# Loading the last two experts' w2 in column halves, and storing half of four output blocks before the second half arrives

## The chip, the cores and the metric

The kernel runs on one core of a Trainium2 chip. The metric is device time in microseconds (us), as the median of many executions. The profile shows one execution; its span is about 1.8 us shorter than the time of the same run (190.8 us of 192.61 us for the kernel before).

The engines have the names of the profile: PE multiplies matrices and leaves the results in PSUM, its accumulator memory; ACT and DVE do elementwise work and copy results out of PSUM (here called evicting); POOL issues the loads and SP the stores, and 16 DMA engines carry both out. In the code, `hp` and `th` are PSUM tiles of the hidden layer, `h_sb` and `hT` its result before and after a transpose, `sop` the slot outputs in PSUM, `slot_oa` the same after the eviction, `cp` and `ob` the combined output before and after its eviction.

## The reference, cut to what matters

Sliding-window attention gives x (4608 tokens by 512 columns). A soft mixture of experts follows: 32 slots, 8 experts with 4 slots each.

```python
logits = x @ phi                        # 4608 x 32
slot_input = softmax(logits, axis=0).T @ x   # needs every token
for e in range(8):                      # w1[e]: 512 x 1024, w2[e]: 1024 x 512
    slot_out[e] = np.maximum(slot_input[e] @ w1[e], 0) @ w2[e]
out = softmax(logits, axis=1) @ slot_out     # 4608 x 512 float32, 9.44 MB
```

So there is one narrow place: the slot inputs need all tokens, the outputs need all experts. Before it the kernel loads q, k, v and 33.6 MB of weights (float32 in HBM, cast to fp16 by the load); after it, it stores 9.44 MB. Everything in this document happens in that narrow place.

## The kernel before

PE builds all 32 slot outputs in one PSUM tile `sop`, evicts it to `slot_oa` in two copies, and then combines: 36 matmuls of 512 columns, each evicted into `ob` by ACT or DVE in turn, with a store for each two of them. Loads are issued by POOL, stores by SP.

```python
def load_w(e, n):                       # n = 0, 1: w1; n = 2, 3: w2, by rows
    ...
    c = slice(4 * n - 8, 4 * n - 4)
    nc.gpsimd.dma_start(out=w2_t[e][:, c], in_=moe_w2[e].rearrange("(c p) d -> p c d", p=128)[:, c])
...
def expert_h(e):                        # hidden layer
    ...                                 # 16 matmuls hp <- slot_inT, w1 (256 columns)
    nc.scalar.activation(h_sb[:, :], hp[:, :], AF.Relu)
    ...                                 # 2 matmuls th: transpose of h
    nc.vector.tensor_copy(out=hT[...], in_=th[:, :])

def expert_o(e):                        # second layer, 8 matmuls of 512 columns
    for i in range(NFC // 4):
        for g in range(4):
            nc.tensor.matmul(sop[32 * g:32 * g + 32, :], hT[:, 4 * i + g, :], w2_t[e][:, 4 * i + g, :],
                             start=(e == 0 and i == 0), stop=(e == E - 1 and i == NFC // 4 - 1))

expert_h(0)
for e in range(E):
    if e + 1 < E:
        expert_h(e + 1)
    expert_o(e)
nc.scalar.copy(out=slot_oa[:, 0:256], in_=sop[:, 0:256])
nc.vector.tensor_copy(out=slot_oa[:, 256:512], in_=sop[:, 256:512])

for blk in range(B + 1):
    ob = pw1.tile([128, 4, D], FP32, name="ob", tag="w1s")
    for g in range(4):
        ...                             # cp <- ET, slot_oa; scaled into ob[:, g, :]
    ...                                 # 2 stores of 512 KB, in rows of 2048 B
```

The softmax here doesn't subtract the row's maximum and nothing guards it: scores larger than these inputs give would overflow.

Of the kernel before, what the change touches and what calls it, by code (L numbers as in the profile page):

```python
# [8 lines left out]
FP32 = mybir.dt.float32  # L9
# [7 lines left out]
def kernel(  # L17
# [10 lines left out]
    nc = tc.nc  # L28

    B, H, S, Dh = q.shape  # L30
    D, NSLOT = moe_phi.shape
    E, _, F = moe_w1.shape
    SPE = NSLOT // E
# [14 lines left out]
    pw1 = ctx.enter_context(tc.tile_pool(name="pw1", bufs=8))  # L48
# [16 lines left out]
        loaded[u] = tiles  # L65

    w1_t, w2_t = {}, {}

    def load_w(e, n):
        if n == 0:  # L70
            w1_t[e] = pw1.tile([128, NHD, F], FP16, name="w1s", tag="w1s")
        if n == 2:
            if e < E - 1:
                w2_t[e] = pw2.tile([128, NFC, D], FP16, name="w2s", tag="w2s")
            else:
                w2_t[e] = pxb.tile([128, NFC, D], FP16, name="w2l", tag="x_bp")
        if n < 2:
            c = slice(2 * n, 2 * n + 2)
            nc.gpsimd.dma_start(out=w1_t[e][:, c], in_=moe_w1[e].rearrange("(c p) f -> p c f", p=128)[:, c])  # L79
        else:  # L80
            c = slice(4 * n - 8, 4 * n - 4)
            nc.gpsimd.dma_start(out=w2_t[e][:, c], in_=moe_w2[e].rearrange("(c p) d -> p c d", p=128)[:, c])  # L82
# [15 lines left out]
    for h in range(2):  # L98
        nc.vector.tensor_copy(
            out=rep[64 * h:64 * h + 64, :, :],  # L100
            in_=ident[64 * h:64 * h + 64, 64 * h:64 * h + 64].unsqueeze(1).broadcast_to([64, 8, 64]))
# [21 lines left out]
    ET = const.tile([128, 4 * B + B // 2, 128], FP16, name="ET")  # L123
# [4 lines left out]
    slot_oa = const.tile([128, D], FP16, name="slot_oa")  # L128
# [178 lines left out]
            nc.vector.tensor_tensor(out=acc[:, :], in0=pa[:, :], in1=acc[:, :], op=ALU.add)  # L307

    nu = len(units)
    w_order = [(e, n) for e in range(E) for n in range(4)]  # L310

    def issue_loads(u):
        if u + 3 < nu:
            load_unit(u + 3)
            for _ in range(2 if u % 3 == 2 else 1):
                load_w(*w_order.pop(0))

    load_w(*w_order.pop(0))
    load_unit(2)
    todo = []  # L320
# [3 lines left out]
    for u in range(nu):  # L324
        issue_loads(u)
        if u == nu - 3:
            while w_order:
                load_w(*w_order.pop(0))
        for j in range(3):
            stage_t2(u, j)  # L330
            stage_s(u, j)
            if u + 1 < nu:
                stage_t1(u + 1, j)
            if pend is not None:
                stage_av(*pend)
                pu, pj = pend
                if pj == 2 and units[pu][1] == 1:
                    b = units[pu][0]
                    todo += [lambda b=b: stage_xt(b, 0), lambda b=b: stage_xt(b, 1), lambda b=b: stage_xt(b, 2),
                             lambda b=b: stage_logit(b), lambda b=b: stage_ex(b), lambda b=b: stage_slot(b)]  # L340
            pend = (u, j)
            if todo:
                todo.pop(0)()
# [18 lines left out]
    ps2 = ctx.enter_context(tc.tile_pool(name="ps2", bufs=2, space=bass.MemoryType.PSUM, reuse_waits="tile"))  # L362
# [3 lines left out]
    nc.vector.tensor_copy(out=slot_inT, in_=si)  # L366

    sel = ident[:, :].rearrange("p (g s) -> p g s", s=NSLOT)
    sop = ps2.tile([128, D], FP32, name="sop", tag="sop", bufs=1)

    def expert_h(e):
        hp = ps2.tile([128, 256], FP32, name="hp", tag="hp")
        for dc in range(NHD):
            for g in range(4):
                nc.tensor.matmul(hp[32 * g:32 * g + 32, :], slot_inT[:, dc, :],
                                 w1_t[e][:, dc, 256 * g:256 * g + 256],
                                 start=(dc == 0), stop=(dc == NHD - 1))
        h_sb = pet.tile([128, 256], FP16, name="h_sb", tag="h_sb")
        nc.scalar.activation(h_sb[:, :], hp[:, :], AF.Relu)
        th = ps2.tile([128, 2, 4, SPE], FP32, name="th", tag="th", bufs=1)  # L380
        for f in range(2):
            nc.tensor.matmul(th[:, f], h_sb[:, 128 * f:128 * f + 128],
                             sel[:, :, SPE * e:SPE * e + SPE], start=True, stop=True)
        hT = hTs[e % 2]
        if e >= 2:
            nc.vector.memset(hT[:, :, SPE * (e - 2):SPE * (e - 2) + SPE], 0.0)
        nc.vector.tensor_copy(
            out=hT[:, :, SPE * e:SPE * e + SPE].rearrange("p (g f) s -> p f g s", f=2), in_=th[:, :])

    def expert_o(e):  # L390
        hT = hTs[e % 2]
        for i in range(NFC // 4):
            for g in range(4):
                nc.tensor.matmul(sop[32 * g:32 * g + 32, :], hT[:, 4 * i + g, :], w2_t[e][:, 4 * i + g, :],
                                 start=(e == 0 and i == 0), stop=(e == E - 1 and i == NFC // 4 - 1))

    expert_h(0)
    for e in range(E):
        if e + 1 < E:
            expert_h(e + 1)  # L400
        expert_o(e)
    nc.scalar.copy(out=slot_oa[:, 0:256], in_=sop[:, 0:256])
    nc.vector.tensor_copy(out=slot_oa[:, 256:512], in_=sop[:, 256:512])

    for blk in range(B + 1):
        ob = pw1.tile([128, 4, D], FP32, name="ob", tag="w1s")
        for g in range(4):
            cp = ps2.tile([128, D], FP32, name="cp", tag="cp", bufs=4)
            nc.tensor.matmul(cp[:, :], ET[:, 4 * blk + g, :], slot_oa[:, :],  # L409
                             start=True, stop=True)  # L410
            cr = crcp[:, blk, g:g + 1] if blk < B else crcp[:, 2 * g + 1, 4:5]
            if g % 2 == 0:
                nc.scalar.activation(ob[:, g, :], cp[:, :], AF.Copy, scale=cr)  # L413
            else:
                nc.vector.tensor_scalar(out=ob[:, g, :], in0=cp[:, :], scalar1=cr, scalar2=None, op0=ALU.mult)  # L415
        if blk < B:
            for g in range(0, 4, 2):
                nc.sync.dma_start(
                    out=out[S * blk + 128 * g:S * blk + 128 * g + 256, :].rearrange("(c p) d -> p c d", p=128),
                    in_=ob[:, g:g + 2, :])  # L420
        else:
            for o in range(2):
                nc.sync.dma_start(
                    out=out.rearrange("(c o t) d -> o t c d", o=2, t=S)[o, 512:576],
                    in_=ob[64 * o:64 * o + 64, :, :])


# [28 lines left out]
```

## Time and profile before

| | before |
|---|---|
| median time, 20 runs | 191.99 us |
| load queue, times of its packets summed | 94.9% of 16 engines' span |
| slot inputs ready (copy starts) | 143.69 us |
| last ReLU starts | 156.50 us |
| last w2 load lands | 158.2 us (issue 138.0, 20.2 us to landing) |
| first store issued | 161.47 us |
| first to last store packet (packet records of the trace) | 26.77 us |

The page's row of 40 slices (each 4.8 us) shows the shape: loads at about 206 GB/s until slice 32, a hole, then stores at about 380 GB/s.

```profile
DMA  4999999999999999999999999999999970999995
GB/s 69 160 201 206 208 207 206 207 210 209 208 206 207 211 206 206 207 207 212 207 205 207 208 208 207 207 211 208 210 207 211 207 118 1 361 375 380 381 339 147
```

The windows view of the kernel before shows the hole closely. Its columns are the window, its length, busy time and instruction count of each engine, then PE's granted clock as a share of the full one, the mean share of the 16 DMA engines and GB/s.

```profile
152.00:154.00 2.00, 1.35 (x32) 0.86 (x28) 0.26 (x2) 0.72 (x2) 0.00 (x0) 1.00 1.16 195
154.00:156.00 2.00, 1.67 (x41) 1.21 (x45) 0.46 (x3) 0.38 (x1) 0.00 (x0) 1.00 0.68 113
156.00:158.00 2.00, 1.51 (x28) 0.55 (x20) 0.26 (x2) 0.38 (x1) 0.00 (x0) 1.00 0.29 47
158.00:160.00 2.00, 0.82 (x6) 0.34 (x6) 0.42 (x1) 0.37 (x1) 0.00 (x0) 0.87 0.00 0
160.00:162.00 2.00, 2.00 (x6) 0.72 (x5) 1.26 (x2) 1.46 (x3) 0.00 (x0) 0.50 0.00 0
162.00:164.00 2.00, 1.80 (x6) 0.59 (x5) 1.82 (x4) 1.83 (x3) 0.00 (x0) 0.78 0.80 297
164.00:166.00 2.00, 1.80 (x7) 0.57 (x6) 2.00 (x4) 1.80 (x4) 0.00 (x0) 1.00 1.02 375
```

From 158 to 162 us nothing moves. The timeline shows what runs in that time (start, length, engine, line, operation, and in brackets how long the engine had been idle and who ended it):

```profile
143.69 0.29 DVE L366 CAST slot_inT<-si 128x128 f16<-128x128 f32 x1 [0.53 <-PE si L365]
...
156.50 0.38 ACT L379 ACTIVATE h_sb<-hp 128x256 f16<-128x256 f32 x1 [1.13 <-PE hp L375]
...
157.19 0.19 DVE L387 CAST hT_143<-th 128x32 f16<-128x32 f32 x1 [1.07 <-PE th L382]
157.44 0.40 PE L394 MATMUL sop<-w2l,hT_143 128*32 128x512 f16 x4
158.25 0.40 PE L394 MATMUL sop<-w2l,hT_143 128*32 128x512 f16 x4 [0.42 <-DMA w2l<-in_moe_w_dram]
158.70 0.37 ACT L402 CAST slot_oa<-sop 128x256 f16<-128x256 f32 x1 [1.81 <-PE sop L394]
159.10 0.42 DVE L403 CAST slot_oa<-sop 128x256 f16<-128x256 f32 x1 [1.72 <-ACT slot_oa L402]
159.58 3.72 PE L409 MATMUL cp<-slot_oa,ET 128*128 128x512 f16 x9 [0.93 <-DVE slot_oa L403]
160.21 0.69 ACT L413 ACTIVATE ob<-cp,crcp 128x512 f32<-128x512 f32 x1 [1.13 <-PE cp L409]
160.63 12.90 DVE L415 TENSOR_SCALAR ob<-cp,crcp 128x512 f32<-128x512 f32 x18 [1.10 <-PE cp L409]
161.47 19.53 SPq L418 DMA_DIRECT2D out_dram<-ob  x16
```

Two things are to be seen. The hole is a chain of short steps: second layer, two evictions one after the other, a combine, two evictions, a store. And PE waited only 0.42 us for the last load.

### The profile page before, as it was taken

To read this page: it belongs to the slowest core of one execution; us is meant where nothing else is said; L and a number is where in the kernel's file an instruction comes from. 1 tells how busy PE (TensorE), PEld (TensorE's weight loads), DVE (VectorE), ACT (ScalarE), POOL (GpSimd) and SP (SyncE) were. 2 spreads that over 40 slices of the span, in tenths; PEclk is the share of its full clock that TensorE was granted. 3 is DMA by queue.
4 is the path that set the end of the run, shared out by engine and by line. 5 is a ranking of instruction groups with operands and counts; after the bars stand their busy time and mean duration, and the time that the engine had idled before them with its cause. 6 is when DMAs were issued, how large, how long until landed. Compare 5 with 4: busy or idle time off the path is not lost.

```text
span 190.8 us, 6583 instructions
## 1 busy us (share of the span) xinstructions
PE 145.2 (76%) x2912; PEld 102.5 (54%) x2912; DVE 109.1 (57%) x259; ACT 112.3 (59%) x189; POOL 59.7 (31%) x89
## 2 busy tenths in 40 slices
PE   0499989999988799899979989988568877881000
PEld 0376767768667676676856876666324442220000
DVE  2116668687667757767766884886841123993000
ACT  2358669769587596766969669666032224992000
POOL 7944534434353434424344433332200000000000
PEclk9999999999999999999999999999955897999555
DMA  4999999999999999999999999999999970999995
GB/s 69 160 201 206 208 207 206 207 210 209 208 206 207 211 206 206 207 207 212 207 205 207 208 208 207 207 211 208 210 207 211 207 118 1 361 375 380 381 339 147
DMA packets 31308, 40.83 MB, mean 214 GB/s; under 512 B 2096, under 2 KB 22576, under 8 KB 31280
## 3 DMA queue, kind: packets, MB, share of 16 engines
q0 software_dynamic: 26384, 30.97, 94.9%
q1 hardware_dynamic: 4896, 9.44, 14.1%
q8 instruction: 23, 0.38, 0.7%
q14 instruction: 5, 0.04, 0.1%
HBM read 61.93 MB, written 9.44 MB: 374 GB/s over the span
## 4 chain that ended last, share of the span: by engine, by line
DMA 31%; PE 26%; ACT 20%; DVE 7%; issue 5%; POOL 1%; DVEq 0%; ACTq 0%; POOLq 0%
DMA w2l<-in_moe_w_dram 11%; DMA w2s<-in_moe_w_dram 9%; ACT pm L197 9%; DMA qn<-in_q_dram 8%; PE tr L143 6%; PE tr L174 5%; DVE ob L415 5%; ACT qT L150 4%; PE sc L185 3%; PE sc L192 3%; DMA kn<-in_k_dram 3%; ACT kT_125 L150 3%; PE av L220 2%; ACT kT_116 L150 2%; PE cp L409 2%
## 5 line engine op out<-in xcount | busy, mean ns | idle before, releaser
L197 ACT ACTIVATE pm<-sc 128x1024 f16<-128x1024 f32 (+1 forms) x48 | 39.5, 822 | 31.0 <-PE sc L192 30.7
L174 PE MATMUL tr<-ident,vT 128*128 128x128 f16 x288 | 24.8, 224 | 1.9 <-DVE rc L226 1.9
L150 ACT COPY qT<-tr 128x640 f16<-128x640 f16 (+1 forms) x32 | 21.8, 743 | 4.2 <-PE tr L143 4.2
L228 DVE TENSOR_TENSOR x_bp<-av,rc 128x512 f16<-128x512 f32 x32 | 21.9, 686 | 0.6
L185 PE MATMUL sc<-rep,hide 64*128 64x512 f16 (+1 forms) x96 | 20.4, 341 | 2.3 <-ACT pm L197 1.8
L174 PEld LDWEIGHTS <-vT 128*128 128x128 f16 x288 | 18.1, 100 | 6.3 <-issue 4.3
L220 PEld LDWEIGHTS <-pm 128*64 128x64 f16 x576 | 15.1, 111 | 7.5 <-issue 6.8
L175 DVE COPY vw_126<-tr 128x1024 f16<-128x1024 f16 (+1 forms) x24 | 13.4, 557 | 7.5 <-PE tr L174 6.7
L143 PE MATMUL tr<-ident,qn 128*64 128x128 f16 x288 | 12.5, 233 | 6.6 <-DMA qn<-in_q_dram 5.2
L60 POOL DMA_DIRECT2D vn<-in_v_dram x16 | 11.5, 716 | 18.5 <-PE av L220 6.4
L82 POOL DMA_DIRECT2D w2s<-in_moe_w_dram x14 | 10.6, 756 | 19.0 <-DMA w1s<-in_moe_w_dram 11.5
L79 POOL DMA_DIRECT2D w1s<-in_moe_w_dram x16 | 11.3, 708 | 16.1 <-DMA w1s<-in_moe_w_dram 7.1
L148 DVE COPY vT<-tr 128x512 f16<-128x512 f16 x16 | 11.6, 724 | 8.2 <-PE tr L143 8.1
L60 POOL DMA_DIRECT2D qn<-in_q_dram x16 | 11.5, 718 | 12.0 <-PE tr L174 3.9
L143 PE MATMUL tr<-ident,vn 128*64 128x128 f16 x288 | 13.0, 227 | 2.8 <-ACT kT_116 L150 1.4
L143 PE MATMUL tr<-ident,kn 128*64 128x128 f16 x288 | 12.0, 228 | 3.5 <-DMA kn<-in_k_dram 2.1
L60 POOL DMA_DIRECT2D kn<-in_k_dram x16 | 11.5, 716 | 9.6 <-PE tr L143 4.3
L226 DVE RECIPROCAL rc<-av 128x8 f32<-128x8 f32 x32 | 6.3, 197 | 14.1 <-PE av L220 14.1
L409 PE MATMUL cp<-slot_oa,ET 128*128 128x512 f16 x36 | 11.7, 431 | 2.3 <-ACT ob L413 1.4
L415 DVE TENSOR_SCALAR ob<-cp,crcp 128x512 f32<-128x512 f32 x18 | 12.6, 748 | 1.4 <-PE cp L409 1.1
L143 PEld LDWEIGHTS <-qn 128*64 128x64 f16 x288 | 9.5, 117 | 7.2 <-DMA qn<-in_q_dram 5.2
L175 DVE COPY vw_118<-tr 128x1024 f16<-128x1024 f16 (+1 forms) x24 | 13.2, 549 | 0.1
(97 smaller groups left out, 261.2 us busy)
## 6 DMA issues: line engine op xcount, KB each, us to landing
out_dram<-ob SPq DMA_DIRECT2D x18, 512.0 KB, 6.0
w1s<-in_moe_w_dram POOLq DMA_DIRECT2D x16, 512.0 KB, 15.1
w2s<-in_moe_w_dram POOLq DMA_DIRECT2D x14, 512.0 KB, 14.0
qn<-in_q_dram POOLq DMA_DIRECT2D x16, 288.0 KB, 13.4
kn<-in_k_dram POOLq DMA_DIRECT2D x16, 288.0 KB, 13.2
vn<-in_v_dram POOLq DMA_DIRECT2D x16, 288.0 KB, 13.2
w2l<-in_moe_w_dram POOLq DMA_DIRECT2D x2, 512.0 KB, 20.1
phi_sb<-in_moe_phi_dram POOLq DMA_DIRECT2D x1, 32.0 KB, 7.8
```

What stands on the lines that cost most here:

```text
L60: nc.gpsimd.dma_start(out=t, in_=src[b, 4 * half:4 * half + 4].rearrange("(x h) (g t) d -> (h g) x (t d)", x=2, h=2, t=T))
L143: nc.tensor.transpose(tr[64 * x:64 * x + 64, j, :], src[:, x, 64 * (t0 + j):64 * (t0 + j) + 64], ident[:, :])
L148: nc.vector.tensor_copy(out=o, in_=i)
L150: nc.scalar.copy(out=o, in_=i)
L174: nc.tensor.transpose(tr[:, 2 * w + h, :], st["vT"][:, h, 64 * i:64 * i + 128], ident[:, :])
L175: nc.vector.tensor_copy(out=st["vw"][:, wins[0]:wins[0] + n, :, 0:64], in_=tr[:, 0:2 * n, :].rearrange("p (w h) (x d) -> p w (h x) d", h=2 ...
L185: nc.tensor.matmul(sc[:, x, 0:128 * n], hide[64 * x:64 * x + 64, :], rep[64 * x:64 * x + 64, 0:2 * n, :], start=True, stop=False, skip_gro ...
L197: nc.scalar.activation(pm[:, :, 0:2 * n, :], sc[:, :, 0:128 * n].rearrange("p x (w q) -> p x w q", q=64), AF.Exp, scale=scale)
L220: nc.tensor.matmul(av[r0:r0 + 64, kk, 65 * (w // 2):65 * (w // 2) + 65], pm[:, x, h * n + w, :], st["vw"][:, i, 2 * h + x, 0:65], start=Tr ...
L228: nc.vector.tensor_tensor(out=xb[:, c0:c0 + 2, 256 * half:256 * half + 256].rearrange("p c (k d) -> p k c d", d=64), in0=avv[:, :, :, 0:64 ...
L409: nc.tensor.matmul(cp[:, :], ET[:, 4 * blk + g, :], slot_oa[:, :], start=True, stop=True)
L415: nc.vector.tensor_scalar(out=ob[:, g, :], in0=cp[:, :], scalar1=cr, scalar2=None, op0=ALU.mult)
```

## The change

The intent is to give the store queue work while the last weights still load. w2 of experts 6 and 7 is loaded by column halves, first halves first. When the first halves are in, half of each slot output is complete, and half of each row of four blocks can be combined and stored.

```diff
+    NLAST = 2
 ...
+        elif e >= E - NLAST:
+            c = slice(D // 2 * (n - 2), D // 2 * (n - 1))
+            nc.gpsimd.dma_start(out=w2_t[e][:, :, c], in_=moe_w2[e].rearrange("(c p) d -> p c d", p=128)[:, :, c])
 ...
-    w_order = [(e, n) for e in range(E) for n in range(4)]
+    w_order = [(e, n) for e in range(E - NLAST) for n in range(4)]
+    last = range(E - NLAST, E)
+    w_order += [(e, n) for e in last for n in range(2)] + [(e, n) for n in range(2, 4) for e in last]
 ...
-    sop = ps2.tile([128, D], FP32, name="sop", tag="sop", bufs=1)
+    sop = [ps2.tile([128, D // 2], FP32, name="sop", tag="sop") for _ in range(2)]
 ...                            # expert_o(e, half): 8 matmuls of 256 columns into sop[half]
                                # combine(blk, cols): combine and store of these columns only
+    NSPLIT = 4
+    whole = slice(0, D)
+    expert_h(0)
+    for e in range(E - NLAST):
+        expert_h(e + 1)
+        expert_o(e, 0)
+        expert_o(e, 1)
+    for e in range(E - NLAST + 1, E):
+        expert_h(e)
+    with tc.manual_schedule(engines={mybir.EngineType.PE, mybir.EngineType.Activation, mybir.EngineType.DVE}):
+        for e in last:
+            expert_o(e, 0)
+        slots_out(0)
+        for blk in range(NSPLIT):
+            combine(blk, halves[0])
+        for e in last:
+            expert_o(e, 1)
+        slots_out(1)
+        for blk in range(NSPLIT):
+            combine(blk, halves[1])
+        for blk in range(NSPLIT, B + 1):
+            combine(blk, whole)
```

(`th` also moves to the PSUM tag of `cp`, with four buffers, and `manual_schedule` keeps the order of the three engines as it is written.) Half rows mean short rows: the last w2 loads write 512 B for each row instead of 1024 B, and the stores of four blocks write 1024 B instead of 2048 B.

More of the change, by code (lines that the diff above doesn't have):

```diff
@@ L379, in expert_h @@
         nc.scalar.activation(h_sb[:, :], hp[:, :], AF.Relu)
-        th = ps2.tile([128, 2, 4, SPE], FP32, name="th", tag="th", bufs=1)
+        th = ps2.tile([128, 2, 4, SPE], FP32, name="th", tag="cp", bufs=4)
         for f in range(2):
@@ L388, in expert_h, with expert_o @@
             out=hT[:, :, SPE * e:SPE * e + SPE].rearrange("p (g f) s -> p f g s", f=2), in_=th[:, :])
-    def expert_o(e):
+    halves = (slice(0, D // 2), slice(D // 2, D))
+    def expert_o(e, half):
         hT = hTs[e % 2]
@@ L393, in expert_o, with slots_out, combine @@
             for g in range(4):
-                nc.tensor.matmul(sop[32 * g:32 * g + 32, :], hT[:, 4 * i + g, :], w2_t[e][:, 4 * i + g, :],
+                nc.tensor.matmul(sop[half][32 * g:32 * g + 32, :], hT[:, 4 * i + g, :],
+                                 w2_t[e][:, 4 * i + g, halves[half]],
                                  start=(e == 0 and i == 0), stop=(e == E - 1 and i == NFC // 4 - 1))
-    expert_h(0)
-    for e in range(E):
-        if e + 1 < E:
-            expert_h(e + 1)
-        expert_o(e)
-    nc.scalar.copy(out=slot_oa[:, 0:256], in_=sop[:, 0:256])
-    nc.vector.tensor_copy(out=slot_oa[:, 256:512], in_=sop[:, 256:512])
-    for blk in range(B + 1):
-        ob = pw1.tile([128, 4, D], FP32, name="ob", tag="w1s")
+    def slots_out(half):
+        if half == 0:
+            nc.scalar.copy(out=slot_oa[:, halves[half]], in_=sop[half])
+        else:
+            nc.vector.tensor_copy(out=slot_oa[:, halves[half]], in_=sop[half])
+    def combine(blk, cols):
+        nd = cols.stop - cols.start
+        ob = pw1.tile([128, 4, nd], FP32, name="ob", tag="w1s")
         for g in range(4):
-            cp = ps2.tile([128, D], FP32, name="cp", tag="cp", bufs=4)
-            nc.tensor.matmul(cp[:, :], ET[:, 4 * blk + g, :], slot_oa[:, :],
-                             start=True, stop=True)
+            cp = ps2.tile([128, nd], FP32, name="cp", tag="cp", bufs=4)
+            nc.tensor.matmul(cp[:, :], ET[:, 4 * blk + g, :], slot_oa[:, cols], start=True, stop=True)
             cr = crcp[:, blk, g:g + 1] if blk < B else crcp[:, 2 * g + 1, 4:5]
@@ L418 @@
                 nc.sync.dma_start(
-                    out=out[S * blk + 128 * g:S * blk + 128 * g + 256, :].rearrange("(c p) d -> p c d", p=128),
+                    out=out[S * blk + 128 * g:S * blk + 128 * g + 256, cols].rearrange("(c p) d -> p c d", p=128),
                     in_=ob[:, g:g + 2, :])
@@ L423 @@
                 nc.sync.dma_start(
-                    out=out.rearrange("(c o t) d -> o t c d", o=2, t=S)[o, 512:576],
+                    out=out.rearrange("(c o t) d -> o t c d", o=2, t=S)[o, 512:576, :, cols],
                     in_=ob[64 * o:64 * o + 64, :, :])
+    NSPLIT = 4
[20 more added lines that the diff above has]
+            combine(blk, whole)
 _INS = ['q', 'k', 'v', 'moe_phi', 'moe_w1', 'moe_w2']
```

## The prediction

> **What bounds the kernel now.** Until about 154 us the load queue: the slice row shows DMA busy at 9 tenths and 206 GB/s in almost every slice. The tail is the store queue: by the windows view 375 to 380 GB/s from 164 to 182 us, while compute ends at 173.5 us and the span at 190.8 us. Between them lies a hole: no DMA traffic from 158 to 162 us. The intent is to fill it by storing half of four blocks while the last weights load.
>
> **Why little of that can happen.** PE, not the load, is nearly last there. By the timeline the slot inputs are ready at 144.0 us, the eight experts run back to back at 1.52 us each (a latency loop: hidden matmuls, ReLU, transpose, copy), and the last hT is copied at 157.4 us. PE's wait on the final w2 load is only 0.42 us (tile view). The first half of the outputs needs all eight hidden layers, so it cannot exist before about 157.8 us, when nearly all loads are done. No real overlap of stores with loads will be seen.
>
> **Gained.** Before: last O matmul ends 158.65, two serial evictions (0.38 us ACT, 0.42 us DVE), first combine matmul 159.58, first store issued 161.47 us. After: O for one half of expert 7 takes about 0.3 us (estimate from the 0.39 us matmuls of 512 columns), no wait on the last load, one eviction, first combine matmul near 158.4, a 128x256 tile evicted in about 0.4 us (as the slot_oa copies) instead of 0.75. First store near 159.4 us: 2 us earlier. The second half (after 16 combine tiles, 3.5 us; O, 0.9 us; an eviction) should issue its first store near 164.7 us, before the first 2 MB drain (about 167 us): no new hole.
>
> **Paid.** Rows are cut in two. From the trace's load packets: 1024 B takes 98 ns, 2048 B 173 ns, so 23 ns fixed plus 0.073 ns per byte; 512 B would take 60 ns, and 4096 of them instead of 2048 of 98 ns cost 2.9 us more on 16 engines (estimate). Loads end near 161 us, before PE needs the second half at about 162 us: hidden. Stores: a 2048 B packet takes 86 ns; with the loads' slope per source byte (0.0366 ns) that is 75 + 11 ns, so 1024 B takes about 49 ns; 4096 of them instead of 2048 at 86 ns cost 1.4 us on the store-bound tail. The Trainium skill, "DMA: Bandwidth & Descriptors", section "Why small descriptors are slow (HBM only)", gives each packet a fixed overhead; the two load sizes agree. Its section "Issuing engines are not separate DMA queues" says that loads and stores share the 16 engines: overlap only moves traffic.
>
> **Sum.** 2.0 us earlier, 1.4 us slower stores, some tenths for late loads: about 0.5 us better. Predicted 191.4 us, range 189.3 to 194.0; faster by over 2%: 7%, within 2%: 87%, slower: 6%.
>
> **What would show each step.** Timeline: first store at 159 to 160 us; the last h-layer copy still near 157.4 us. DMA packets: 512 B loads near 60 ns, 1024 B stores near 49 ns; last weight load near 161 us. Windows: the 4 us hole shrinks to 2 us or less; under 350 GB/s for the first 4 MB of stores, 380 after. Stores end near 189 us.
>
> **What would make it wrong.** Slower: 1 KB stores well above 49 ns (60 ns adds 3 us), or store issue (0.4 us unblocked) limiting them; PE waiting on the second half, if load and store packets share engines unfairly. Faster: a hidden-layer loop sped up by half-width O matmuls and th in four buffers.

## The result, and the profile after

The changed kernel takes 191.37 us (median of 10 runs, 190.36 to 192.77) against 191.99 us (20 runs). The ratio is 0.9964, 95% interval 0.9939 to 0.9990: a real gain, of about 0.7 us (0.36% of 192 us). A ratio here is the mean time of one kernel's fast runs over that of the other's of the same rounds, so it is not quite the ratio of the two medians. Executions over 1.5% slower than the fastest of the same kernel are left out of the means.

The two profiles differ by more (spans of 190.8 and 188.2 us), and part of that isn't the change's: in the changed kernel's trace the slot inputs were ready at 142.34 us instead of 143.69 us, before anything changed has run on PE. In the experiments below that moment lies between 142.2 and 144.9 us, with no order by kernel. So times in this document are read from that copy on. (The expectations count from its end, 0.29 us later.) Where a step waits for a load this is not quite fair, because the loads do not start from that copy.

The windows of the changed kernel:

```profile
152.00:154.00 2.00, 1.68 (x52) 1.33 (x56) 0.46 (x3) 0.39 (x1) 0.00 (x0) 1.00 1.47 196
154.00:156.00 2.00, 1.26 (x34) 0.70 (x26) 0.26 (x2) 0.46 (x2) 0.00 (x0) 1.00 1.03 140
156.00:158.00 2.00, 1.65 (x8) 0.93 (x8) 0.99 (x3) 1.51 (x4) 0.00 (x0) 0.58 0.50 71
158.00:160.00 2.00, 1.86 (x9) 0.83 (x8) 1.75 (x4) 1.78 (x5) 0.00 (x0) 0.57 0.78 256
160.00:162.00 2.00, 1.35 (x23) 0.75 (x22) 1.44 (x4) 0.74 (x3) 0.00 (x0) 1.00 1.03 340
```

The hole is gone: no window is empty, though the DMA share dips to 0.50. But it was not filled by overlap. By the packet records, the stores start as the last few load packets end, in the same microsecond (first store packet at 158.50 us, last load packet at 158.38 us). And the first stores run at 340 GB/s where those of before ran at 375 to 380. The timeline, with the same steps as before:

```profile
142.34 0.29 DVE L372 CAST slot_inT<-si 128x128 f16<-128x128 f32 x1 [0.51 <-PE si L371]
...
154.54 0.39 ACT L385 ACTIVATE h_sb<-hp 128x256 f16<-128x256 f32 x1 [1.14 <-PE hp L381]
...
155.23 0.19 DVE L393 CAST hT_143<-th 128x32 f16<-128x32 f32 x1 [1.07 <-PE th L388]
155.47 0.40 PE L402 MATMUL sop<-w2l,hT_143 128*32 128x256 f16 x8 [0.28 <-DVE hT_143 L393]
155.93 0.37 ACT L408 CAST slot_oa<-sop 128x256 f16<-128x256 f32 x1 [1.00 <-PE sop L402]
156.35 4.22 PE L417 MATMUL cp<-slot_oa,ET 128*128 128x256 f16 x16 [0.47 <-ACT slot_oa L408]
157.55 10.44 SPq L425 DMA_DIRECT2D out_dram<-ob  x15
...
160.50 0.40 PE L402 MATMUL sop<-w2s,hT_141 128*32 128x256 f16 x8
```

PE no longer waits for a load here (the wait of the last second-layer matmuls is now on hT), and the second half at 160.50 us does not wait either. What the first half does wait for is the hidden layers. They run as slowly as before.

| us after the slot input copy | before | after |
|---|---|---|
| last ReLU starts | 12.81 | 12.20 |
| first store issued | 17.78 | 15.21 |
| from last ReLU to first store | 4.97 | 3.01 |
| first to last store packet | 26.77 | 28.06 |

The first store comes 2.6 us earlier. Of this, 2.0 us lie between the last ReLU and the store, in the part that the change rewrote. By the two timelines the second layer before the first eviction takes 0.8 us less (0.46 instead of 1.26 us, and 0.42 of that was the wait for the load), one eviction instead of two saves 0.5 us (0.42 instead of 0.88), and the narrower combine and its evictions 0.7 us (1.20 instead of 1.89). The other 0.6 us lie in the expert loop, and the windows view shows PE's clock at 0.50 until 148 us in the kernel before and only until about 146 us in the changed one, so the first experts ran at half clock for longer. The clock records of the five traces with this expert loop sort them: with half clock until 5.5 and 5.3 us after the slot inputs (before, store_halves) the last ReLU comes after 12.81 and 12.80 us, with half clock until 3.7, 3.2 and 3.1 us (the changed kernel, row_loads, load_halves) after 12.20, 12.05 and 11.99 us. load_halves has the unchanged compute, so those 0.6 us aren't the half-width matmuls' doing. The Trainium skill, "TensorE: Matmul & The Clock Gate", section "Part 1: The HAM clock gate (the "warmup" mystery)", says that the gate's window runs free, so that where it opens varies from run to run. The trace agrees: the granted clock reads 0.50 or 1.00, and a hidden matmul of 256 columns takes 421 ns at most and 273 ns in the median. Against the gain stand 1.3 us of a longer store stretch. 2.0 minus 1.3 is 0.7 us, what the runs show (their interval is 0.2 to 1.2 us).

So close an agreement of two single traces with the mean of many runs is luck. The way from the last ReLU to the first store is not the same in each execution: store_halves below computes it as the kernel before does, and took 3.95 us where before took 4.97. Its last load was in before PE needed it, and its combine ran at full clock, while the combine of before and of the changed kernel ran at half clock.

### The profile page after: what moved, and what is told of

Same layout as the page of the kernel before. It is cut to its first block, busy times and chain, and to the rows that moved or that the text cites. A ratio compares the mean times of both kernels' runs of the same rounds, so it can differ in the third digit from the quotient of the medians.

```text
span 188.2 us, 6791 instructions
## 1 busy us (share of the span) xinstructions
PE 143.7 (76%) x2992; PEld 103.7 (55%) x2992; DVE 110.7 (59%) x267; ACT 114.5 (61%) x197; POOL 60.3 (32%) x89
## 4 chain that ended last, share of the span: by engine, by line
PE 44%; ACT 32%; issue 6%; DVE 6%; DMA 3%; POOL 0%; ACTq 0%; POOLq 0%
ACT pm L201 12%; PE tr L147 7%; PE tr L178 7%; ACT qT L154 5%; PE sc L189 5%; PE sc L196 5%; ACT ob L420 4%; ACT kT_125 L154 4%; PE av L224 4%; DMA kn<-in_k_dram 3%; PE cp L417 3%; ACT kT_116 L154 3%; PE pa L306 3%; PE hp L381 3%; PE tr L261 3%
## 5 line engine op out<-in xcount | busy, mean ns | idle before, releaser
L147 PE MATMUL tr<-ident,qn 128*64 128x128 f16 x288 | 12.0, 227 | 6.6 <-DMA qn<-in_q_dram 5.3
L422 DVE TENSOR_SCALAR ob<-cp,crcp 128x256 f32<-128x256 f32 (+1 forms) x26 | 14.4, 585 | 2.7 <-PE cp L417 2.5
L60 POOL DMA_DIRECT2D qn<-in_q_dram x16 | 11.5, 718 | 13.9 <-PE tr L147 4.7
L420 ACT ACTIVATE ob<-cp,crcp 128x256 f32<-128x256 f32 (+1 forms) x26 | 13.8, 556 | 2.3 <-PE cp L417 1.9
L417 PE MATMUL cp<-slot_oa,ET 128*128 128x256 f16 (+1 forms) x52 | 12.9, 341 | 2.8 <-ACT ob L420 0.6
L147 PE MATMUL tr<-ident,kn 128*64 128x128 f16 x288 | 12.2, 228 | 3.7 <-DMA kn<-in_k_dram 1.8
L86 POOL DMA_DIRECT2D w2s<-in_moe_w_dram x12 | 9.1, 757 | 15.0 <-DMA w1s<-in_moe_w_dram 11.7
```

Source lines behind the costliest of these rows:

```text
L60: nc.gpsimd.dma_start(out=t, in_=src[b, 4 * half:4 * half + 4].rearrange("(x h) (g t) d -> (h g) x (t d)", x=2, h=2, t=T))
L147: nc.tensor.transpose(tr[64 * x:64 * x + 64, j, :], src[:, x, 64 * (t0 + j):64 * (t0 + j) + 64], ident[:, :])
L417: nc.tensor.matmul(cp[:, :], ET[:, 4 * blk + g, :], slot_oa[:, cols], start=True, stop=True)
L420: nc.scalar.activation(ob[:, g, :], cp[:, :], AF.Copy, scale=cr)
L422: nc.vector.tensor_scalar(out=ob[:, g, :], in0=cp[:, :], scalar1=cr, scalar2=None, op0=ALU.mult)
```

## The experiments

The experiments were run in three sittings on three chips (up to hidden_pipelined; before_pipelined to pipelined_nsplit1; the two wide ones), and each sitting timed the kernel before again. Ratios are the safe comparison between sittings.

Two theories were tested. Theory 1, the prediction's: the hidden layers on PE set when the first half exists, so there is nothing to store while the weights load; the short rows then take back most of what the shorter chain gains. Theory 2: the loads set the end. The short rows make the last load late, on the engines that finish last, and a faster PE would change nothing.

| run | loads | hidden layers | blocks split | ratio to before | 95% interval | median us |
|---|---|---|---|---|---|---|
| the change | column halves | as before | 4 | 0.9964 | 0.9939 to 0.9990 | 191.37 |
| store_halves | rows | as before | stores only | 1.0087 | 1.0058 to 1.0116 | 194.04 |
| load_halves | column halves | as before | 0 | 1.0052 | 1.0019 to 1.0085 | 193.37 |
| row_loads | rows | as before | 4 | 1.0005 | 0.9978 to 1.0032 | 192.56 |
| hidden_pipelined | column halves | pipelined | 4 | 0.9838 | 0.9796 to 0.9879 | 189.16 |
| before_pipelined | rows | pipelined | 0 | 1.0019 | 0.9988 to 1.0050 | 192.44 |
| pipelined_row_loads | rows | pipelined | 4 | 1.0027 | 0.9996 to 1.0058 | 192.61 |
| pipelined_nsplit2 | column halves | pipelined | 2 | 0.9839 | 0.9810 to 0.9867 | 189.07 |
| pipelined_nsplit1 | column halves | pipelined | 1 | 0.9927 | 0.9899 to 0.9954 | 190.63 |
| pipelined_wide_o | column halves | pipelined, wide | 4 | 0.9798 | 0.9770 to 0.9826 | 188.12 |
| pipelined_wide_o_nsplit3 | column halves | pipelined, wide | 3 | 0.9767 | 0.9738 to 0.9796 | 187.41 |

All gave correct results.

### store_halves: the cost of short stores by itself

```diff
-                nc.sync.dma_start(out=out[..., :], in_=ob[:, g:g + 2, :])
+                for c in ((slice(0, D // 2), slice(D // 2, D)) if blk < 4 else (slice(0, D),)):
+                    nc.sync.dma_start(out=out[..., c], in_=ob[:, g:g + 2, c])
```

> The kernel before, with nothing changed but that the output of blocks 0 to 3 is stored in two column halves (1024 B rows instead of 2048 B). It measures one cost by itself. The accounting theory (the tail is bound by store packets: 4096 of 48.9 ns in place of 2048 of 86 ns, over 16 engines) expects the stretch from first to last store packet to grow by 1.3 to 1.5 us and the time by as much, about 193.4 us. A rival, that the tail is bound by something that does not count packets (bytes to HBM, or the wait for the last receipts), expects no change, 192.0 us. If the issue of twice as many stores (0.4 us each) limited it, more than 3 us would be added.

Measured: ratio 1.0087, 1.7 us more. The packet records give 46 ns in the median for a 1024 B store packet (mean 48.7) and 86 ns for one of 2048 B; the stretch from first to last store packet grew from 26.77 to 28.23 us. The store stage ran at the rate that the changed kernel shows:

```profile
162.00:164.00 2.00, 1.65 (x6) 0.57 (x6) 2.00 (x4) 1.90 (x4) 0.00 (x0) 1.00 1.02 343
```

So the cost is real, it lies in the packets, and twice as many issues did not add to it.

### load_halves: the cost of short loads by itself

Only the `load_w` and `w_order` parts of the change, on the kernel before.

> The kernel before, with nothing changed but the loads: w2 of the last two experts in column halves and in the new order; compute and stores as before, so that PE needs both halves. The accounting theory expects the last weight to land later by up to 2.9 us (4096 packets of 60.2 ns in place of 2048 of 98.3 ns over 16 engines), with the span longer by about 2 to 2.5 us since PE waited only 0.4 us for the last load before: 194 to 194.5 us. The rival, that the hidden layers on PE set the end of the stage and loads have slack, expects under 1 us.

Measured: ratio 1.0052, 1.0 us more, where 2 to 2.5 us were expected. PE starved, twice: it waited 1.9 us for w2 of expert 6 and 0.84 us for that of expert 7, and then worked at half clock. The first of these waits comes from the order of the loads as well as from the short rows: the second half of expert 6 is now issued after the first half of expert 7.

```profile
155.94 1.01 PE L400 MATMUL sop<-w2s,hT 128*32 128x512 f16 x5 [1.89 <-DMA w2s<-in_moe_w_dram]
...
158.49 1.05 PE L400 MATMUL sop<-w2l,hT 128*32 128x512 f16 x8 [0.84 <-DMA w2l<-in_moe_w_dram]
```

But the last load landed at about 158.5 us, barely later than the 158.2 us of before. Over all traces, the last load packet ends at 157.0 to 158.0 us in the five kernels with row loads and at 157.9 to 158.8 us in the seven with column halves, 0.75 us later in the mean. The predicted delay of 2.9 us came from adding up packet times, and those overlap. In the windows of the changed kernel the DMA share reads 1.47 at 196 GB/s, in those of before from 146 to 152 us 1.15 to 1.18 at 206 to 210: a share over 1 says that an engine had more than one packet under way. The rate is what counts: 197 GB/s against 206 in full windows. For the 2.1 MB of these loads that is about 0.5 us (10.65 against 10.18 us, an estimate from the two rates).

### row_loads: the loads undone in the changed kernel

> The changed kernel with the loads undone: w2 in row halves and in the order of before; compute and stores split as changed. The first half of the outputs then needs the last load whole. Theory 1 (PE readiness sets the first store in the changed kernel, loads had slack only because the first column halves came early): O of expert 7 waits about 1 to 1.5 us for the load, the first store is issued about 16 us after the slot inputs' hidden layers begin, against 14.9 in the changed kernel and 17.4 before; with 1.3 us for the smaller stores the time is that of before, 191.6 to 192.4 us. Theory 2 (the late loads of the slowest DMA engines set the end in the changed kernel, and 512 B rows made them later): the loads end 2 us earlier and the time is 1 us or more better than the changed kernel, 190.0 us or less.

Measured: ratio 1.0005, as theory 1 had it; theory 2 wanted 190.0 us or less. The first store came 16.7 us after the slot inputs (15.2 in the changed kernel). PE waited for the last load:

```profile
156.36 0.29 PE L398 MATMUL sop<-w2l,hT 128*32 128x256 f16 x4 [0.28 <-DVE hT L389]
158.34 0.29 PE L398 MATMUL sop<-w2l,hT 128*32 128x256 f16 x4 [1.69 <-DMA w2l<-in_moe_w_dram]
```

So the column halves are needed for the gain, even though no store runs beside them: they take the last load off the chain.

### hidden_pipelined: a faster hidden loop

The hidden matmuls of expert e+2 go before the transpose of e+1, so PE has work while ACT does the ReLU. `expert_h` is cut in two at the ReLU, and the loop, too, now runs in the order as written (`manual_schedule`).

```diff
+    with tc.manual_schedule(engines={mybir.EngineType.PE, mybir.EngineType.Activation, mybir.EngineType.DVE}):
+        expert_h1(0)
+        expert_h1(1)
+        expert_h2(0)
+        for e in range(E - NLAST):
+            expert_h1(e + 2)
+            expert_h2(e + 1)
+            expert_o(e, 0)
+            expert_o(e, 1)
+        expert_h2(E - 1)
```

> The changed kernel with the hidden layers of the eight experts software-pipelined on PE (the hidden matmuls of expert e+2 before the transpose of e+1, so that PE does not wait for ReLU), nothing else. All hidden layers should be done 2 to 3 us earlier. Theory 1 (PE's latency loop delays the first half, and so the stores): the first store is issued 1.5 to 3 us earlier and the time falls by 1.5 to 2.5 us, to about 189 us. Theory 2 (loads of 512 B rows end at about 159 us on the slowest engines whatever PE does, and their stores queue behind or among them): stores start earlier but the time falls by less than 0.7 us against the changed kernel, 190.7 us or more.

Measured: ratio 0.9838, so 2.4 us better than the change (0.9838 over 0.9964 is 0.9874). Theory 1 holds and theory 2 falls: the last load was issued at 138.1 us and took up to 20.3 us, landing at about 158.4 us, much as before, and yet the time fell. The last ReLU starts 10.0 us after the slot inputs instead of 12.2 (although half clock lasted longer here, until 5.3 us), the first store is issued after 13.9 us instead of 15.2. That is less than the ReLU's gain because PE stood still for 0.9 us for a reason that the profile does not name ("issue"); more on this under pipelined_wide_o.

```profile
143.14 0.29 DVE L372 CAST slot_inT<-si 128x128 f16<-128x128 f32 x1 [0.53 <-PE si L371]
...
153.07 0.51 PE L408 MATMUL sop<-w2s,hT 128*32 128x256 f16 x12
153.11 0.38 ACT L387 ACTIVATE h_sb<-hp 128x256 f16<-128x256 f32 x1 [0.74 <-PE hp L383]
...
154.49 0.29 PE L408 MATMUL sop<-w2s,hT 128*32 128x256 f16 x4 [0.91 <-issue]
...
157.08 5.82 SPq L431 DMA_DIRECT2D out_dram<-ob  x9
```

The store's start explains 1.3 us of the 2.4; the rest is not settled by this trace (the interval of the ratio is 0.8% wide, 1.6 us).

### before_pipelined: does the loop gain by itself?

The same pipelining on the kernel before.

> The kernel before with only the pipelined hidden layers (no halves anywhere). It asks whether the gain of hidden_pipelined (ratio 0.984) is the loop's own or needs the split. If the loads set the end of the stage in the kernel before (last weight lands at 158.2 us, PE waited 0.42 us for it), a faster loop only makes PE wait longer: 191.5 to 192.5 us, the wait on the last w2 load growing from 0.4 to 2 us or more. Rival: the loop alone is worth its 2 to 3 us in any kernel: about 189.5 us.

Measured: ratio 1.0019, no gain. The last hT was copied 10.3 us after the slot inputs instead of 13.5, and PE waited the time away, 2.65 us in two waits:

```profile
155.13 0.40 PE L400 MATMUL sop<-w2l,hT 128*32 128x512 f16 x4 [0.50 <-DMA w2l<-in_moe_w_dram]
157.68 0.40 PE L400 MATMUL sop<-w2l,hT 128*32 128x512 f16 x4 [2.15 <-DMA w2l<-in_moe_w_dram]
```

### pipelined_row_loads: the loads undone under the faster loop

> hidden_pipelined with the loads undone (w2 in row halves, order of before). If the column halves of the loads are what makes the first half ready early, PE now waits for the whole last w2 (lands about 158.3 us), the first store goes back to about 160 us, and the time to that of row_loads: 192 to 192.8 us. Rival: once PE is fast the load split is worth no more than the 1 us it seemed worth with the slow loop: about 190.2 us.

Measured: ratio 1.0027, all of the 3 us gone. With the two runs before it, this makes a square:

| split compute, ratio to before | hidden layers as before | pipelined |
|---|---|---|
| w2 by rows | 1.0005 | 1.0027 |
| w2 by column halves | 0.9964 | 0.9838 |

Neither the early half nor the fast loop does much alone. There were two limits at almost the same time, 0.42 us apart, and taking away one leaves the other.

### pipelined_nsplit2 and pipelined_nsplit1: fewer blocks split

`NSPLIT` 2 and 1 instead of 4 in hidden_pipelined.

> hidden_pipelined with two blocks split instead of four: 2048 stores of 1024 B fewer pairs, so the store stretch shortens by half of the 1.3 to 1.7 us that store_halves measured, 0.65 to 0.85 us. The first half of two blocks (1 MB) drains in 3.1 us, by about 161.5 us; the second half can issue near 160.5, its packets start near 161.8: a hole of at most 0.5 us. Expected 188.3 to 189.0 us, against 189.2 of hidden_pipelined. If the hole is larger than that, no gain.

> hidden_pipelined with one block split. Saves three quarters of the cost of short rows, 1.0 to 1.25 us, but 0.5 MB drains in 1.6 us, by about 160 us, while the second half waits for the last load (158.5 us) and its packets start near 161.8: a hole of 1.5 to 2 us. Expected 0.3 to 0.8 us slower than pipelined_nsplit2, about as hidden_pipelined. If the time keeps falling instead, the hole is hidden by something not seen.

Measured: nsplit2 has the ratio of hidden_pipelined (0.9839 and 0.9838); the gain expected of it did not show, though its store stretch was shorter by 0.5 us (27.46 against 27.97 us). No hole is the reason: the longest time between two store packets is 0.09 us. With intervals of 0.6 to 0.8%, and the two kernels run on different chips, such a gain can hide; it stays open. nsplit1 is slower by 0.9% (0.9927), more than expected, and for the reason expected: the second half cannot start before its load is in (PE waited 0.8 us for it), and half a megabyte does not last that long. PE also ran at half clock just then. The hole is back, in the middle of the stores, 1.38 us without a store packet:

```profile
160.00:162.00 2.00, 1.76 (x6) 0.83 (x7) 1.09 (x3) 1.09 (x3) 0.00 (x0) 0.50 0.43 149
```

So the first half must hold enough stores to last until the second is ready.

### pipelined_wide_o and pipelined_wide_o_nsplit3: PE's standstill, and the best kernel

The first six experts never needed halves. Here they run in 512-column matmuls on one accumulator again; the last two keep halves.

```diff
+    sop = ps2.tile([128, D], FP32, name="sop", tag="sop", bufs=1)
 ...
-            expert_o(e, 0)
-            expert_o(e, 1)
+            expert_o(e, slice(0, D))
```

> hidden_pipelined, but the first six experts' second layer runs in full 512-column matmuls on one accumulator, as before the change (96 PE rows fewer: 48 matmuls and 48 weight loads); the last two experts still in halves. In the three pipelined traces with half-width second layers PE stands still for 0.6 to 0.9 us with no releaser that the profile shows, always after the same 12th second-layer matmul of expert 5. If that standstill hangs on the place in PE's instruction stream (fetch of instructions), it moves or goes, and where it goes the first store comes up to 0.9 us earlier after the slot inputs (13.6 us in hidden_pipelined): about 188.4 us. If it is a wait for data (weights of expert 5 or a buffer), it stays at the same matmuls and the time is 189.2 us.

> The same with three blocks split. The store stretch is shorter by 0.3 to 0.4 us (a quarter of what store_halves cost), and the 1.5 MB of first halves drain in 4.7 us, which covers the second half's way to its first store (about 4.4 us in hidden_pipelined for four blocks, less for three). Expected 0.3 us faster than pipelined_wide_o, about 188.1 us; equal if a hole opens.

Measured: 0.9798 and, with three blocks split, 0.9767. The standstill is gone; the first store is issued 12.0 and 12.5 us after the slot inputs, 2.9 us after the last ReLU in both, where hidden_pipelined took 4.0 us. Three blocks were expected to gain 0.3 us over four and gained 0.6 us by the ratios, but the intervals overlap. In all four half-width pipelined traces it had come after the same matmul of expert 5, for 0.6 to 1.0 us: 5805 records of PE's matmuls and weight loads stand before it in each. The weights of expert 5 are loaded in the same way here, and before_pipelined, with wide matmuls, does not have it. The four matmuls after it also read a load that four matmuls before it had already read for the other half. So it wasn't a wait for these data. It belongs to the place or the number of PE's instructions. That it is the fetch of instructions is only argued: the Trainium skill, "Runtime: NRT & Kernel Launch", section "Instruction fetch mechanics", says that each engine's instructions are streamed in blocks of 16 KiB by a DMA queue of their own, the cost mostly hidden. The traces do show packets of 16384 B on the instruction queue, of 0.88 to 1.05 us each in the narrow place, and in all four traces one of them begins 1.4 to 1.6 us before the standstill; but it ends 0.5 to 0.75 us before it, and the wide kernels have such packets too, without a standstill.

Here the intended overlap is at last there. The windows of pipelined_wide_o_nsplit3, to be held against those of before and after:

```profile
154.00:156.00 2.00, 1.36 (x8) 0.77 (x8) 1.18 (x3) 1.64 (x5) 0.00 (x0) 1.00 0.96 129
156.00:158.00 2.00, 1.27 (x13) 0.50 (x12) 1.49 (x4) 1.32 (x4) 0.00 (x0) 1.00 1.07 271
158.00:160.00 2.00, 1.00 (x12) 0.60 (x12) 0.71 (x2) 0.40 (x2) 0.00 (x0) 1.00 1.06 356
160.00:162.00 2.00, 1.73 (x9) 0.87 (x9) 1.70 (x5) 1.79 (x6) 0.00 (x0) 0.79 0.97 332
```

Between 156 and 158 us loads and stores run side by side (packet records: 222 load packets of 512 B and 418 store packets of 1024 B start in it), and the DMA share never falls under 0.96 in these windows. Its slices show the same:

```profile
DMA  4999999999999999999999999999999999999996
```

PE now waits 0.80 us for the second half of the last load (at 158.30 us), so the two limits meet again: more from here would have to come from the loads.

## Why the prediction was right

- **The size and the sign.** Predicted 191.4 us and about 0.5 us better; measured 191.37 us and about 0.7 us, with an interval of 0.2 to 1.2 us. That the sign and the order of size came out is the account below; that the two figures agree to a tenth is luck.
- **"Why little of that can happen."** Right, and shown by experiment. The first half waits for the hidden layers: speeding them up moved the first store and the time (hidden_pipelined, 0.9838), and only in the kernel with column halves.
- **"Gained": first store 2 us earlier.** From the last ReLU to the first store it was 4.97 us and became 3.01 us. The trace shows 2.6 us in all, but 0.6 us of it are the clock's. The 2 us come from the one trace of the kernel before; with the 3.95 us of store_halves in its place they would be 0.9 us, so the term is known less well than the prediction made it look. "No new hole" held: the ninth store, the first of the second half, was issued at 162.71 us and the first 2 MB lasted until 164.67 us.
- **"Paid", stores.** 49 ns for a 1024 B store packet were predicted and 48.9 were measured in the mean; 1.4 us longer were predicted and 1.3 us were measured (1.5 us of stretch and 1.7 us of time in store_halves). The 49 ns were worked out from the median of the long packets, 86 ns, and the median of the short ones is 46 ns; like for like, in means, the first 4.19 MB have packets of 48.9 ns instead of 88.7 ns and took 12.30 instead of 11.18 us, so the short rows themselves cost 1.1 us here. It takes back two thirds of the gain.
- **"Paid", loads.** This term was mis-sized. The packet time was right (60 ns, measured 60.2), the sum of the packet times was not a duration: "Loads end near 161 us" was wrong. The last w2 landed at 158.7 us in the changed kernel (issue 138.4, up to 20.3 us to landing), half a microsecond later than before, instead of 2.9 us. The error did no harm because the prediction had counted the delay as hidden; in load_halves, where it would not have been hidden, the same error gave an expectation twice too high. For stores the same sum works, since their share reads 1.02 to 1.04: nearly one packet at a time.
- **What it did not see.** It named the latency loop but not what followed: that loop and last load were so close that the change pays little until the loop is shortened too, and then, with two smaller mends, pays 4.5 us of 192 (0.9767).

Left open: why nsplit2 did not gain over four blocks when three blocks seem to, in the wide kernel (the intervals of the two wide kernels overlap); what PE's standstill was; whether the shorter way to the first store (one eviction, a narrower combine) could be had without short rows, which no run tried; and whether some DMA engines end their loads later than others. The falling rate from 154 to 158 us would fit the last, but the trace does not name the engine of a packet.

## What to carry to other kernels

When a stage waits for two things that come at almost the same time, easing one of them earns little: look at how long the wait on the last one is (here 0.42 us) before you expect more than that, and shorten both. To overlap stores with loads, ask first when the first storable result can exist, not when its data arrive. Price short rows from the packet records, but check the DMA share first: where it reads over 1 packet times overlap and their sum is not time, so use the GB/s.

## What the Trainium skill lacked or had wrong

- "DMA: Bandwidth & Descriptors" gives no trn2 rate for stores by row size (the store rates that it lists by row size are not for trn2). Here 1024 B rows ran at 340 GB/s (46 ns a packet in the median), 2048 B rows at 380 GB/s (86 ns).
- The same page, section "Why small descriptors are slow (HBM only)", explains the loss by about 3 cycles per packet, and by 32 B of descriptor metadata for each operation. Estimated from that, with 32 B per cycle (64 + 3 against 32 + 3 cycles), 1024 B rows would lose about 4%, and under 6% with one more cycle for the metadata; the runs show about 10% (340 of 380 GB/s). The direction agrees, the size does not.
- It gives no figure for how far the packet times of loads overlap. With 512 B rows they sum to 1.47 of 16 engines at 196 GB/s, with 1024 and 2048 B rows to 1.15 to 1.18 at 206 to 210 GB/s, so that halving the rows cost 4 to 7% of the rate and not the 18% that the packet times say (98.3 over 2 times 60.2 ns is 0.82).
- "Runtime: NRT & Kernel Launch", section "Instruction fetch mechanics", calls the fetch mostly hidden. No run here disproves it, but PE stood still for 0.6 to 1.0 us at one fixed place of its instruction stream in every half-width pipelined kernel, with no releaser in the profile, and no page tells how to recognise such a stop.
